# A Conformer block on one core: gated unit and convolution repacked as 128 + 16 channels, whole-chunk norms, and PSUM pairs reserved for ScalarE

## The chip, the core and the metric

The kernel runs on one core of a Trainium2 chip. The metric is device time in microseconds (us), as the median of a few executions. The engines are called as in the profile: PE is TensorE's matmuls, PEld its weight loads, DVE is VectorE, ACT is ScalarE, POOL is GpSimd.

Ratios are the mean time of one kernel's fast runs over that of the other's of the same rounds, so they are not quite the ratio of the medians quoted beside them.

## The reference

Two sequences of 4000 tokens with 144 channels go through one block, all in bf16:

```python
h = layernorm(x);  x = x + 0.5 * (silu(h @ w_ff1a) @ w_ff1b)          # 144 -> 576 -> 144
q, k, v = split(layernorm(x) @ w_qkv)                                  # 4 heads of 36
x = x + softmax(q @ k.T * 36**-0.5) @ v @ w_o                          # full attention, 4000 keys
a, b = split(layernorm(x) @ w_pw1)                                     # 144 + 144
c = depthwise_conv5(a * sigmoid(b), dw)                                # per channel, along tokens
x = x + silu(c) @ w_pw2
x = x + 0.5 * (silu(layernorm(x) @ w_ff2a) @ w_ff2b)
return layernorm(x)
```

## The kernel before

Tokens are cut into 16 chunks of 500 (eight for each sequence), and a chunk into four blocks of 125. Token `4p + i` of a chunk sits at position p of block i. Attention runs through 1008 **tiles**: 16 chunks of queries times 63 tiles of 64 keys, all four heads at once. A tile is one group of four score matmuls (128 partitions x 1000 columns of PSUM, two neighbouring banks), one exponential, and one group of four value matmuls.

An exponential is one ScalarE instruction over both banks, or, for some tiles, eight VectorE instructions that build the same from shifts and a polynomial. Of the eight PSUM banks two hold the attention's output, so six are shared by score tiles, which need a **pair**, and by all other work, which takes one bank at a time.

The order of instructions is fixed when the kernel is built. A recording layer keeps its own rough estimate of when each engine would be free, and a scheduler picks the next step from it; on the chip each engine then simply goes through its list, with semaphores. Three stages follow. The *start* runs up to the first exponential (first feed-forward, keys and values of the first chunk). The *body* is the stream of 1008 tiles, with the rest of the block filled in between. The *tail* comes after the last exponential.

The parts that the change touches (cuts marked):

```python
HD = 72                                   # 144 channels as two halves of 72 partitions
class Banks(Slots):
    def take(self):                       # one bank for any other work: anything nearly free
        t = min(self.free.values()) + 0.3
        ok = [i for i, f in self.free.items() if f <= t]
        i = min(ok, key=lambda j: ((j ^ 1) in self.free, self.free[j], j))
        del self.free[i]
        return i
    def take_pair(self): ...              # two neighbouring banks for a score tile

def ln_tr(c, s, g):                       # half a chunk (2 blocks): norm, transpose, copy
    u = yield from ln(c, g)
    yield from transp(XN[0:TB, u, :, :], ("XN", u), XT[0:HD, s, :, g*2*TB:(g+1)*2*TB], [("XT", s, g)])

def glu(c, s, hf):                        # spawned for hf = 0, 1
    bk, t = yield need("pe", (banks, thp), dur=0.42)
    mm2(WP1, s, D + hf * HD, D + (hf + 1) * HD, bk, HD, ["WP1"])      # 72 outputs x 500 tokens
    yield from tanh(bk, t, HD)                                        # 72x500 on ScalarE
    ...
    mm2(WP1, s, hf * HD, (hf + 1) * HD, bk, HD, ["WP1"])
    op("dve", "scalar_tensor_tensor", out=U[0:HD, c % NU, hf, :, 1:1 + TB], ...)   # 72x500

def conv(c, z, hf, silu):                 # spawned for hf = 0, 1: nine diagonal matmuls, 72 channels
    ...
    op("pe", "matmul", o[:, i0:i1, :], lhsT=DG[0:HD, hf, tap, :], rhs=u[:, s0:s0 + i1 - i0, off:off + TB], ...)
    yield from tanh(bk, t, HD)

def want_dve(n):                          # does VectorE take this tile's exponential?
    if not DVE_EXP or live_dve[0] >= 1 or t > NT - 6 or (t < 3 and c == 0) or len(kv_done) < CPB:
        return False
    return R.free["dve"] < R.free["pe"] + 0.6
```

The softmax here doesn't subtract the row's maximum and nothing guards it: scores larger than these inputs give would overflow.

## Time and profile before

| | busy, us | share of the 1075.4 us span |
|---|---|---|
| TensorE matmuls | 957.5 | 89% |
| VectorE | 913.5 | 85% |
| ScalarE | 938.5 | 87% |
| GpSimd | 363.6 | 34% |

The median time was 1079.0 us (three executions). The table does not name a bottleneck: three engines stand within 4 points. The next lines do. First, from the page of the kernel before: the busy share of ScalarE in 40 equal slices (tenths), and the shares of engines and lines in the chain of work that ended last.

```profile
ACT  3998789999889998999879899999999999999932
...
ACT 37%; PE 33%; DVE 16%; POOL 11%; issue 2%; DMA 1%; ACTq 0%; POOLq 0%; DVEq 0%
PE PS L155 33%; ACT PT L155 31%; POOL RS L155 6%; POOL XN L155 4%; ACT TH L155 4%; DVE ZB L155 4%; DVE MB L155 2%; DVE ST L155 2%; DVE X L155 2%; DVE HT L155 1%; DVE OTF L155 1%; DVE SW L155 1%; DMA WQKV<-in_w_qkv_dram 1%; DVE XT L155 1%; DVE PT L155 1%
```

The body is nearly full and both ends are not, so an average over the span mixes stages. The view of busy time by windows, cut at the first and after the last exponential (busy us, with the number of instructions in brackets; PEclk is TensorE's granted clock):

```profile
core 0: us, PE busy (x) PEld busy (x) DVE busy (x) ACT busy (x) POOL busy (x), PEclk, DMA share, GB/s
0.00:33.51 33.51, 27.98 (x212) 15.17 (x212) 24.00 (x126) 16.67 (x30) 12.96 (x35) 1.00 0.33 99
33.51:1025.63 992.12, 896.35 (x10796) 341.47 (x10797) 865.52 (x2153) 909.13 (x1095) 339.13 (x646) 0.99 0.01 4
1025.63:1075.40 49.77, 33.15 (x194) 21.80 (x191) 24.02 (x94) 12.71 (x22) 11.56 (x27) 0.63 0.03 10
```

ScalarE is busy 909.1 of the 992.1 us of the body, 91.6%, so it is idle for 83 us there. The groups of instructions (busy us, mean ns of one | idle us of the engine just before them and what ended it):

```profile
L155 ACT ACTIVATE PT<-PS 128x1000 bf16<-128x1000 f32 x885 | 829.1, 1024 | 76.4 <-PE PS L155 73.9
...
L155 DVE TENSOR_TENSOR PT<-ZB,MB 128x1000 bf16<-128x1000 bf16 x123 | 84.9, 690 | 2.9
...
L155 ACT ACTIVATE TH<-PS 128x500 bf16<-128x500 f32 x112 | 65.2, 612 | 1.0 <-PE PS L155 0.8
...
L155 ACT ACTIVATE TH<-PS 72x500 bf16<-72x500 f32 x60 | 35.2, 586 | 3.9 <-PE PS L155 3.8
```

ScalarE computes 885 tiles and VectorE 123 (the second line is the last of its eight instructions). 76.4 us of ScalarE's idle time stand before exponentials. The view of waits says for whom (us in total, times, longest us):

```profile
ACT PT L155 <- PE PS L155: 73.9, 121, 2.3
...
PE PS L155 <- ACT PT L155: 44.3, 154, 1.1
...
PE PS L155 <- POOL XN L155: 26.4, 32, 2.4
```

They wait for score matmuls. TensorE also waits for ScalarE, in the other direction: a new score tile needs a pair of banks that an exponential has not yet freed. And it waits 26.4 us for norms that GpSimd computes (`XN`).

TensorE's 89% is not a sign of a full engine. The Trainium skill (Perfetto Trace Analysis, "Identifying the Most-Contended Engine") says that the busy share of matmuls is a poor measure of how near the engine is to its limit, because they are pipelined, and points to the arithmetic rate and to the share of weight loads instead. This trace agrees with the first half: the matmuls of a score group show 392 ns each, but the timeline has the next group starting 0.21 to 0.24 us after the group's own start, as here:

```profile
645.60 0.41 PE L155 MATMUL PS<-QT,KT 64*64 64x500 bf16 x4
...
645.83 0.38 PE L155 MATMUL PS<-PT,VA 64*37 64x500 bf16 x4
```

The weight loads are busy for 35% of the span.

### The profile page before, as it was taken

To read this page: it belongs to the slowest core of one execution; us is meant where nothing else is said; L and a number is where in the kernel's file an instruction comes from. 1 tells how busy PE (TensorE), PEld (TensorE's weight loads), DVE (VectorE), ACT (ScalarE), POOL (GpSimd) and SP (SyncE) were. 2 spreads that over 40 slices of the span, in tenths; PEclk is the share of its full clock that TensorE was granted. 3 is DMA by queue.
4 is the path that set the end of the run, shared out by engine and by line. 5 is a ranking of instruction groups with operands and counts; after the bars stand their busy time and mean duration, and the time that the engine had idled before them with its cause. 6 is when DMAs were issued, how large, how long until landed. Compare 5 with 4: busy or idle time off the path is not lost.

```text
span 1075.4 us, 26861 instructions
## 1 busy us (share of the span) xinstructions
PE 957.5 (89%) x11198; PEld 378.4 (35%) x11198; DVE 913.5 (85%) x2372; ACT 938.5 (87%) x1147; POOL 363.6 (34%) x707
## 2 busy tenths in 40 slices
PE   8999989999999999998989998898989898888866
PEld 4444333333333344323433332223332333323244
DVE  6867988889989898888988999988889898878844
ACT  3998789999889998999879899999999999999932
POOL 4312343425442546223254153113123142324112
PEclk9999999999999999999999999999999999999966
DMA  4000000000000000000000000000000000000000
GB/s 124 2 2 1 2 2 1 2 2 5 4 2 2 7 2 7 4 5 2 1 7 7 1 7 5 4 1 7 2 2 7 2 7 1 7 2 8 1 6 12
DMA packets 8996, 7.32 MB, mean 7 GB/s; under 512 B 2298, under 2 KB 8874, under 8 KB 8874
## 3 DMA queue, kind: packets, MB, share of 16 engines
q1 hardware_dynamic: 7718, 5.13, 1.6%
q8 instruction: 88, 1.44, 0.6%
q10 hardware_dynamic: 1156, 0.47, 0.2%
q14 instruction: 34, 0.28, 0.1%
HBM read 3.30 MB, written 2.30 MB: 5 GB/s over the span
## 4 chain that ended last, share of the span: by engine, by line
ACT 37%; PE 33%; DVE 16%; POOL 11%; issue 2%; DMA 1%; ACTq 0%; POOLq 0%; DVEq 0%
PE PS L155 33%; ACT PT L155 31%; POOL RS L155 6%; POOL XN L155 4%; ACT TH L155 4%; DVE ZB L155 4%; DVE MB L155 2%; DVE ST L155 2%; DVE X L155 2%; DVE HT L155 1%; DVE OTF L155 1%; DVE SW L155 1%; DMA WQKV<-in_w_qkv_dram 1%; DVE XT L155 1%; DVE PT L155 1%
## 5 line engine op out<-in xcount | busy, mean ns | idle before, releaser
L155 ACT ACTIVATE PT<-PS 128x1000 bf16<-128x1000 f32 x885 | 829.1, 1024 | 76.4 <-PE PS L155 73.9
L155 PE MATMUL PS<-QT,KT 64*64 64x500 bf16 x4032 | 411.8, 392 | 46.8 <-ACT PT L155 31.6
L155 PE MATMUL PS<-PT,VA 64*37 64x500 bf16 x4032 | 373.8, 375 | 16.6 <-ACT PT L155 11.8
L155 POOL TENSOR_SCALAR RS<-MV 125x2 f32<-125x2 f32 x276 | 93.1, 337 | 573.7 <-DVE MV L155 559.2
L155 PEld LDWEIGHTS PS<-QT,KT 64*64 64x64 bf16 x4032 | 122.3, 104 | 295.1 <-ACT PT L155 197.4
L155 DVE TENSOR_SCALAR ZB<-PS 128x500 uint16<-128x500 f32 x246 | 154.7, 670 | 18.6 <-PE PS L155 17.3
L155 POOL TENSOR_SCALAR XN<-X,RS 125x144 bf16<-125x144 bf16 x232 | 136.2, 593 | 12.1
L155 PEld LDWEIGHTS PS<-PT,VA 64*37 64x37 bf16 x4032 | 106.1, 96 | 92.0 <-ACT PT L155 53.5
L155 POOL TENSOR_TENSOR RS<-RS,NHALF 125x2 f32<-125x2 f32 x160 | 127.6, 797 | 13.3
L155 ACT ACTIVATE TH<-PS 128x500 bf16<-128x500 f32 (+2 forms) x200 | 110.8, 575 | 5.6 <-PE PS L155 5.2
L155 DVE SCALAR_TENSOR_TENSOR HT<-TH,PS 128x500 bf16<-128x500 bf16 (+1 forms) x140 | 84.3, 616 | 30.4 <-ACT TH L155 29.4
L155 DVE TENSOR_SCALAR MB<-MB 128x1000 f16<-128x1000 f16 x246 | 102.3, 416 | 2.5
L155 DVE TENSOR_TENSOR PT<-ZB,MB 128x1000 bf16<-128x1000 bf16 x123 | 84.9, 690 | 2.9
L155 DVE TENSOR_TENSOR MB<-MB 128x1000 f16<-128x1000 f16 x123 | 83.3, 678 | 2.8
L155 PE MATMUL PS<-IDENT,XN 125*72 125x125 bf16 x512 | 52.1, 227 | 34.6 <-POOL XN L155 26.4
L155 DVE SCALAR_TENSOR_TENSOR X<-PS,X 125x288 bf16<-125x288 f32 x128 | 56.4, 449 | 26.7 <-PE PS L155 25.9
L155 DVE BATCH_NORM_STATS2 ST<-X 125x6 f32<-125x144 bf16 x320 | 77.4, 293 | 0.3
L155 PE MATMUL PS<-XT,WA 72*128 72x500 bf16 x256 | 73.9, 393 | 1.7 <-DVE HT L155 0.7
L155 DVE COPY XT<-PS 72x500 bf16<-72x500 bf16 x119 | 48.2, 410 | 31.0 <-PE PS L155 29.9
L155 PE MATMUL PS<-WB,HT 128*125 128x144 bf16 x640 | 61.3, 237 | 2.3 <-ACT HT L155 1.9
L155 PEld LDWEIGHTS PS<-IDENT,XN 125*72 125x72 bf16 x512 | 34.3, 115 | 77.0 <-POOL XN L155 49.7
L155 PE MATMUL PS<-U,DG 72*72 72x250 bf16 (+3 forms) x288 | 58.8, 311 | 1.8 <-POOL U L155 1.5
(68 smaller groups left out, 710.5 us busy)
## 6 DMA issues: line engine op xcount, KB each, us to landing
X<-in_x_dram SPq DMA_DIRECT2D x16, 140.6 KB
out_dram<-XN SPq DMA_DIRECT2D x32, 70.3 KB
WA<-in_w_ff1a_dram ACTq DMA_DIRECT2D x1, 144.0 KB
WB<-in_w_ff1b_dram ACTq DMA_DIRECT2D x1, 144.0 KB
WA<-in_w_ff2a_dram SPq DMA_DIRECT2D x1, 144.0 KB
WB<-in_w_ff2b_dram SPq DMA_DIRECT2D x1, 144.0 KB
WQKV<-in_w_qkv_dram ACTq DMA_DIRECT2D x1, 121.5 KB
WP<-in_w_pw_dram SPq DMA_DIRECT2D x1, 81.0 KB
```

The lines of the kernel that those rows point to most:

```text
L155: ins = getattr(eng, o.name)(*o.a, **o.k)
```

## The change

Its intent is to take work off ScalarE, VectorE and TensorE around the gated unit and the convolution, to shorten the instruction lists of norms and transposes, and to let nothing else take the PSUM pairs that keep ScalarE fed. Its core (cuts marked):

```diff
-def glu(c, s, hf):   ... 72 channels x 500 tokens, twice
+def glu(c, s):       # 128 channels x 500 tokens
+    mm2(WP1, s, D, D + ML, bk, ML, ["WP1"])
+    yield from tanh(bk, t, ML)
+    ...
+def glu_left(c, s):  # the 16 channels left over: block i lands on partitions 16i..16i+15
+    for ab in (1, 0):
+        for i in range(NB):
+            for k in range(2):
+                op("pe", "matmul", PSV[0:LP, bk, (1 - ab) * 128:(1 - ab) * 128 + TB],
+                   lhsT=WPZ[0:HD, k, ab, 48 - LC * i:128 - LC * i],     # weights between zeros
+                   rhs=XT[0:HD, s, k, i * TB:(i + 1) * TB], ...)
+    yield from tanh(bk, t, LP, TB)                                       # 80 partitions x 125
...
-def conv(c, z, hf, silu):   nine matmuls for each half of 72
+def conv(c, z, silu):       nine matmuls for 128 channels
+def conv_left(c, z, silu):  three matmuls of 125 columns: taps between blocks are in the weights
...
-def ln_tr(c, s, g):         half a chunk
+def ln_tr(c, s, bs):        parts(): whole chunks in the body, halves in start and tail
+    NXN = 5                 # buffers of a whole chunk; before: 8 of half a chunk
...
 class Banks(Slots):
+    def choose(self):       # a single bank only while two pairs are free or queued for ScalarE
+        ok = [i for i in self.free if self.pairs(i) + len(self.queued) >= self.keep]
+        ...
+        return min((i for i in ok if self.free[i] <= t), key=lambda j: (-self.pairs(j), self.free[j], j))
...
-            return ok[0]
+            return min(ok, key=lambda q: not q[2].req.hold)   # first what holds a bank or a buffer
...
+def lag():   # pacing: is other work behind the attention? then no tile for VectorE, and LATE more room
+    ...
 def want_dve(n):
-    return R.free["dve"] < R.free["pe"] + 0.6
+    return len(eq) + banks.pairs() >= KEEP and R.free["dve"] < R.free["pe"] + DSLACK and not lag()
+KEEP = 2; DSLACK = 0.6; PRELAG = 0.5; BMIN = 1.5; DRAIN = 0.6; LATE = 0.3; DGAP = 5.0
+def reserve():   # a third pair when a tile for VectorE is due (5 us after its last one)
```

Also changed: in the scheduler's model, the latency of the score matmuls and the costs of the value projections and of the norm's steps on VectorE and GpSimd; ranks of threads, one buffer instead of two for VectorE's tiles, five instead of two for attention outputs, the order of the four value matmuls, and the projection after the convolution (one matmul of 128 channels and one of the stacked 16 for each block, instead of two of 72).

## The prediction

> **What bounds the kernel now.** The page: TensorE 89%, VectorE 85%, ScalarE 87% of 1075.4 us. Cut by stage (busy time by windows), ScalarE is busy 16.7 of 33.5 us up to its first softmax exponential, 909.1 of the next 992.1 us (91.6%), and 12.7 of the last 49.8. The body is a stream of 1008 attention tiles: ScalarE takes 885 (one exponential 1024 ns, 937 ns of engine time), VectorE 123 (530 us, 4.3 us each). ScalarE is the bound; its 83 us idle in the body is the loss, nearly all exponentials waiting for score matmuls (waits: 73.9 us, 121 times). TensorE is busy on paper, but matmuls overlap: from issue intervals in the timeline (attention group of four 0.21 us, feed-forward matmul 0.21) I estimate 770 us of 992. It is late because other work holds PSUM pairs or because VectorE (865.5 of 992 in the body) frees banks late, not for lack of capacity.
>
> **What the change does**, by counting instructions of both programs:
> - ScalarE: 29 tiles come back from VectorE (885 to 914; VectorE 123 to 94). 500-wide tanh fall from 172 to 138, 30 of 125 columns are added, five silu go to the tail. For widths the trace lacks I use the Trainium skill (ScalarE: Activation LUTs, "What ACT_TABLE_LOAD costs"): 186 ns + 0.833 ns per column, about 93 ns of overlap; that gives 1019 ns for 1000 columns, the trace 1024. So +29 x 0.93, -34 x 0.50, +30 x 0.19, +2: **+17 us of ScalarE**, 938 to about 955.
> - VectorE: -29 x 4.3 = -125 us; 60 combining passes of 500 columns (0.67 us) become 30 of 500 and 30 of 125: -12; whole-chunk copies: about -9. **About -145 us**, 85% to about 73%.
> - TensorE: gated-unit and conv matmuls go from 72 to 128 output channels at the same cost, so the main parts halve; the 16 left over add 304 matmuls of 125 columns. Estimate -15 us, and 490 bursts of other work between attention groups instead of 518.
> - GpSimd: 145 instructions fewer; not critical.
> - Scheduling: single PSUM banks are given out only while two pairs are free or queued for ScalarE.
>
> So ScalarE's work grows. The gain can only come from its idle time: reserved pairs and a VectorE with a quarter of slack should let TensorE run ahead. I expect the body's ScalarE share to rise from 91.6% to about 95.5%: 921 us busy (some tanh move to the ends) / 0.955 = 964 us. The start stays near 35 us, the tail near 49 (half the conv matmuls, but one more chunk's feed-forward). Sum 1048; I predict **1046 us** (range **1024 to 1073**). Chances: faster by over 2% 0.68, within 2% 0.27, slower 0.05.
>
> **What would show it.** ScalarE busy 945 to 962 us; idle before exponentials from 76 to 25-45 us; VectorE near 73%; tanh 80x125 near 275 ns; body about 28 us shorter; tail within 3 us. In the chain of waits, ScalarE's share rises above 37%. If VectorE's relief is the cause, TensorE's waits on VectorE shrink; if the pairs are, its waits on exponentials shrink.
>
> **What would make it wrong.** (1) The order is fixed ahead by the kernel's own model; if its latencies are off, ScalarE stays near 92%: about 1079 us or more. (2) Two banks left for all else could starve the feed-forward chains and push work into the tail. (3) ScalarE above 97%: near 1030 us. (4) Whole-chunk norms lengthen chains; harmless unless the last chunks wait for them.

## The result and the profile after

| | before | after |
|---|---|---|
| median, us | 1079.7 (4 runs) | 1030.6 (4 runs, 1028.1 to 1031.8) |
| ratio | | 0.9543 (95%: 0.9516 to 0.9569) |
| start: up to the first exponential, us | 33.5 | 37.7 |
| body, us | 992.1 | 929.3 |
| ScalarE busy in the body, us (share) | 909.1 (91.6%) | 911.0 (98.0%) |
| ScalarE idle in the body, us | 83.0 | 18.3 |
| tail, us | 49.8 | 59.3 |
| tiles on ScalarE / VectorE | 885 / 123 | 914 / 94 |

The kernel became 49 us faster, and its output was correct. From the page of the changed kernel, the same lines as of before:

```profile
ACT  3899999999999999999999999999999999999741
...
ACT 65%; PE 22%; DVE 9%; POOL 2%; issue 1%; DMA 1%; ACTq 0%; POOLq 0%; DVEq 0%
ACT PT L158 59%; PE PS L158 22%; ACT TH L158 5%; DVE ZB L158 2%; DVE ST L158 1%; DVE MB L158 1%; DVE HT L158 1%; POOL RS L158 1%; DVE X L158 1%; POOL XN L158 1%; DMA WQKV<-in_w_qkv_dram 1%; DVE XT L158 1%; DVE PT L158 0%; DVE XN L158 0%; DVE MV L158 0%
```

The view of busy time by windows, cut in the same way:

```profile
core 0: us, PE busy (x) PEld busy (x) DVE busy (x) ACT busy (x) POOL busy (x), PEclk, DMA share, GB/s
0.00:37.69 37.69, 30.78 (x246) 17.27 (x246) 27.98 (x131) 18.24 (x34) 13.60 (x35) 1.00 0.31 89
37.69:966.99 929.30, 856.63 (x10822) 323.80 (x10822) 732.42 (x1852) 910.99 (x1112) 255.77 (x494) 1.00 0.01 4
966.99:1026.30 59.31, 37.43 (x229) 23.98 (x226) 27.63 (x110) 16.59 (x31) 13.97 (x34) 0.64 0.03 8
```

The groups of instructions, and after them the waits:

```profile
L158 ACT ACTIVATE PT<-PS 128x1000 bf16<-128x1000 f32 x914 | 851.9, 1041 | 11.5 <-PE PS L158 9.8
...
L158 ACT ACTIVATE TH<-PS 128x500 bf16<-128x500 f32 x138 | 84.1, 616 | 6.0 <-PE PS L158 5.7
...
L158 DVE TENSOR_TENSOR PT<-ZB,MB 128x1000 bf16<-128x1000 bf16 x94 | 66.0, 702 | 2.2
...
L158 ACT ACTIVATE TH<-PS 80x125 bf16<-80x125 f32 x30 | 8.6, 288 | 1.5 <-PE PS L158 1.5
```

```profile
PE PS L158 <- ACT PT L158: 37.9, 135, 1.0
...
ACT PT L158 <- PE PS L158: 9.8, 30, 1.0
...
PE PS L158 <- POOL XN L158: 2.0, 3, 1.0
```

ScalarE did *more* in the body than before, 911.0 against 909.1 us, and the body still lost 62.8 us. All of that is idle time: exponentials that waited 73.9 us for scores now wait 9.8. The chain of waits says the same: its share on ScalarE went from 37% to 65%, that of TensorE's PSUM groups from 33% to 22%.

Some of the gain went back at the ends: the start is 4.2 us longer and the tail 9.5 us. The sum is 4.2 - 62.8 + 9.5 = -49.1 us, the difference of the two spans.

The tail can be read further. The groups in the tail's window alone, first of the kernel before, then of the changed one:

```profile
L155 ACT ACTIVATE HT<-PS 128x500 bf16<-128x500 f32 x8 | 4.5, 587 | 4.7 <-PE PS L155 4.7
```

```profile
L158 ACT ACTIVATE HT<-PS 128x500 bf16<-128x500 f32 x12 | 7.0, 587 | 5.3 <-PE PS L158 5.2
```

Twelve full-width feed-forward activations stand in the tail instead of eight: a third chunk's second feed-forward was left over. The granted clock in the tail is 0.64 against 1.00 in the body; it was 0.63 before, so the clock is no reason for the tail's growth. The Trainium skill (TensorE: Matmul & The Clock Gate, "The HAM clock gate") says that the clock of TensorE is throttled by default and that sustained activity releases it; the traces agree, with 0.63 and 0.64 in tails where TensorE is busy for 67 and 63% of the time, and 0.99 to 1.00 in bodies where it is busy for 90 and 92%.

### The profile page after: what moved, and what is told of

The parts are those of the page before. It is cut to its first block, busy times and chain, and to the rows that moved or that the text cites. A ratio compares the mean times of both kernels' runs of the same rounds, so it can differ in the third digit from the quotient of the medians.

```text
span 1026.3 us, 26612 instructions
## 1 busy us (share of the span) xinstructions
PE 924.8 (90%) x11294; PEld 365.0 (36%) x11294; DVE 788.0 (77%) x2092; ACT 945.8 (92%) x1175; POOL 283.3 (28%) x562
## 4 chain that ended last, share of the span: by engine, by line
ACT 65%; PE 22%; DVE 9%; POOL 2%; issue 1%; DMA 1%; ACTq 0%; POOLq 0%; DVEq 0%
ACT PT L158 59%; PE PS L158 22%; ACT TH L158 5%; DVE ZB L158 2%; DVE ST L158 1%; DVE MB L158 1%; DVE HT L158 1%; POOL RS L158 1%; DVE X L158 1%; POOL XN L158 1%; DMA WQKV<-in_w_qkv_dram 1%; DVE XT L158 1%; DVE PT L158 0%; DVE XN L158 0%; DVE MV L158 0%
## 5 line engine op out<-in xcount | busy, mean ns | idle before, releaser
L158 ACT ACTIVATE PT<-PS 128x1000 bf16<-128x1000 f32 x914 | 851.9, 1041 | 11.5 <-PE PS L158 9.8
L158 PE MATMUL PS<-QT,KT 64*64 64x500 bf16 x4032 | 397.4, 391 | 50.3 <-ACT PT L158 29.5
L158 POOL TENSOR_SCALAR RS<-MV 125x4 f32<-125x4 f32 (+1 forms) x160 | 46.3, 289 | 668.3 <-DVE MV L158 662.7
L158 DVE TENSOR_SCALAR ZB<-PS 128x500 uint16<-128x500 f32 x188 | 118.5, 672 | 33.2 <-PE PS L158 31.9
L158 POOL TENSOR_TENSOR RS<-RS,NHALF 125x4 f32<-125x4 f32 (+1 forms) x103 | 97.6, 948 | 8.6
L158 DVE TENSOR_SCALAR MB<-MB 128x1000 f16<-128x1000 f16 x188 | 78.0, 415 | 1.5
L158 DVE TENSOR_TENSOR PT<-ZB,MB 128x1000 bf16<-128x1000 bf16 x94 | 66.0, 702 | 2.2
L158 DVE TENSOR_TENSOR MB<-MB 128x1000 f16<-128x1000 f16 x94 | 63.8, 679 | 2.1
L158 PEld LDWEIGHTS PS<-WB,HT 128*125 128x125 bf16 x640 | 49.4, 143 | 37.4 <-issue 22.6
L158 DVE COPY XT<-PS 72x1000 bf16<-72x1000 bf16 (+1 forms) x65 | 40.1, 617 | 11.7 <-PE PS L158 10.6
```

The costliest lines, as they stand in the source:

```text
L158: ins = getattr(eng, o.name)(*o.a, **o.k)
```

## The experiments

The profile shows *that* ScalarE is fed, not which part of the change feeds it. The theories:

- **A**: the two reserved pairs of PSUM banks do it; TensorE can always run ahead.
- **B**: the relief of VectorE does it (94 tiles instead of 123, 913.5 down to 788.0 us busy): banks that VectorE must free come back sooner.
- **C**: the packing of gated unit and convolution, the whole-chunk norms and the new priorities do it.

Every kernel gave the right output. Each was run four times; the kernel before, run beside them on the same chips, had medians of 1077.8 to 1079.7 us, and the ratios are to those runs. "Body" and "tail" are cut as above; the share is ScalarE's in the body.

| run | median, us | ratio to before | start | body | share | idle | tail | tiles on VectorE |
|---|---|---|---|---|---|---|---|---|
| before | 1079.7 | 1 | 33.5 | 992.1 | 91.6% | 83.0 | 49.8 | 123 |
| changed | 1030.6 | 0.9543 | 37.7 | 929.3 | 98.0% | 18.3 | 59.3 | 94 |
| 1 no reservation | 1039.2 | 0.9631 | 45.4 | 944.9 | 94.2% | 55.0 | 46.9 | 127 |
| 2 the same, fewer VectorE tiles | 1049.6 | 0.9730 | 47.2 | 954.7 | 95.8% | 40.3 | 46.6 | 96 |
| 3 before, fewer VectorE tiles | 1077.0 | 0.9982 | 34.8 | 992.4 | 93.7% | 63.0 | 49.1 | 97 |
| 4 before, reservation alone | 1070.1 | 0.9927 | 35.4 | 983.4 | 95.4% | 45.0 | 47.7 | 80 |
| 5 changed, old conv | 1055.0 | 0.9778 | 40.1 | 948.2 | 97.3% | 25.2 | 65.3 | 89 |
| 6 changed, half-chunk norms | 1038.0 | 0.9629 | 37.5 | 937.2 | 97.4% | 24.7 | 61.7 | 93 |
| 7 changed, no "holders first" | 1043.0 | 0.9667 | 40.7 | 941.3 | 97.1% | 27.3 | 62.0 | 93 |
| 8 before, new conv alone | 1069.2 | 0.9917 | 35.5 | 985.8 | 91.3% | 85.8 | 45.0 | 124 |
| 9 changed, LATE 0.15 | 1021.5 | 0.9474 | 39.6 | 934.4 | 98.4% | 15.3 | 47.4 | 85 |
| 10 changed, tuned a | 1018.5 | 0.9450 | 34.8 | 932.3 | 98.3% | 15.9 | 47.5 | 88 |
| 11 changed, tuned b | 1015.3 | 0.9417 | 37.2 | 931.5 | 98.4% | 14.5 | 46.9 | 89 |
| 12 changed, no pacing | 1046.6 | 0.9693 | 38.9 | 926.7 | 96.8% | 29.7 | 79.6 | 103 |

### 1. The changed kernel without the reservation

```diff
-    KEEP = 2
+    KEEP = 0
-        return KEEP + 1 if due else KEEP
+        return KEEP
```

With `KEEP` at 0 VectorE's tiles need no free pairs either, and no third pair is kept for them.

> The changed kernel with the reservation of PSUM pairs switched off, nothing else edited; by count VectorE then takes 127 of the 1008 tiles (94 in the changed kernel), ScalarE 881. Theory A (the two reserved pairs keep ScalarE fed): ScalarE's share of the body, 98.0% in the changed kernel, falls back to 91 to 94%, the waits of exponentials for score matmuls grow from 9.8 to over 40 us, and with 31 us less ScalarE work than the changed kernel the time is 1040 to 1065 us. Rival B (the relief of VectorE did it): also slower, because VectorE gets its 33 tiles back and is busy again 85% or more; same numbers. Rival C (packed conv, whole-chunk norms and priorities did it): ScalarE stays at 97% or more and the time is at or under 1030 us.

The body in the view by windows (columns as above), then the group of exponentials:

```profile
45.35:990.24 944.89, 865.26 (x10826) 336.13 (x10824) 852.50 (x2108) 889.91 (x1082) 265.99 (x494) 1.00 0.01 4
```

```profile
L158 ACT ACTIVATE PT<-PS 128x1000 bf16<-128x1000 f32 x881 | 824.0, 1032 | 52.3 <-PE PS L158 50.7
```

ScalarE's share fell to 94.2% and its waits for scores rose from 9.8 to 50.7 us, as theory A said. But the whole kernel lost only 8.6 us (1030.6 to 1039.2), which is just under A's range of 1040 to 1065. Without the reservation VectorE took 33 tiles more, which saved ScalarE 21 us of work in the body (889.9 against 911.0). So most of the 49 us does *not* depend on the reservation. With the rest alone the kernel is already 40 us under the one before, although C's numbers (a share of 97% or more, 1030 us at most) were wrong. The stages moved in different directions: start 7.7 us longer (at a granted clock of 0.86 instead of 1.00), body 15.6 us longer, tail 12.4 us shorter, without the third chunk's feed-forward in it.

### 2. The same, with VectorE's tiles limited

```diff
-        ... < R.free["pe"] + DSLACK and not lag()
+        ... < R.free["pe"] + DSLACK and not lag() and R.free["pe"] > last_dve[0] + 8.0
```

(on top of the edit of run 1)

> As the run before, without reservation, but VectorE may take a tile only 8 us after its last one: 96 tiles, nearly the 94 of the changed kernel, so VectorE has the same slack and ScalarE the same work. Theory A (pairs): ScalarE's share of the body stays at 92 to 95%, body 960 to 990 us, time 1050 to 1080 us. Rival B (VectorE's slack): share 97 to 98%, body 930 to 940 us, time 1018 to 1035 us. Rival C: as B.

```profile
47.24:1001.98 954.74, 869.83 (x10839) 331.66 (x10839) 732.73 (x1862) 914.46 (x1114) 252.65 (x494) 1.00 0.01 4
```

That is the body's row. With VectorE's load as in the changed kernel (732.7 against 732.4 us in the body) ScalarE stays at 95.8%, not at 98.0%. B's range (1018 to 1035 us) is missed by far; A's time (1050 to 1080) by 0.4 us, its share (at most 95%) by 0.8 points and its body (at least 960 us) by 5.3 us. At nearly equal division of tiles, the reservation is worth 25 us of the body and 19 us of the kernel, for the start is 9.5 us longer without it (clock 0.89) and the tail 12.7 us shorter.

### 3. The kernel before, with VectorE's tiles limited

```diff
-        return R.free["dve"] < R.free["pe"] + 0.6
+        return R.free["dve"] < R.free["pe"] + 0.6 and R.free["pe"] > last_dve[0] + 8.0
```

> The kernel before, with VectorE limited in the same way to 97 tiles instead of 123, so ScalarE gets 26 more exponentials (24 us). Rival B (VectorE's slack feeds ScalarE): the body's share rises from 91.6% to 96 to 98%, time 1030 to 1050 us, faster than before. Theory A: share at most 94%, the added work is not paid back, time 1075 to 1100 us. VectorE falls from 85% to about 75% of the span either way.

```profile
34.80:1027.22 992.42, 897.71 (x10806) 340.56 (x10807) 766.05 (x1947) 929.45 (x1121) 324.71 (x646) 0.99 0.01 4
```

VectorE's work in the body fell from 865.5 to 766.1 us and the body's length did not move (992.1, 992.4). ScalarE's idle time fell by 20 us, from 83.0 to 63.0, and its work rose by the same 20 us, from 909.1 to 929.5. The median moved by 1.8 us, and the interval of the ratio (0.9952 to 1.0012) contains 1. B is refuted as a cause that works alone: slack on VectorE does feed ScalarE better, but it is bought with the tiles that ScalarE has to take over.

### 4. The kernel before, with the reservation alone

```diff
+    (choose(), pairs(), queued, keep as in the change)
+        banks.keep = 2            # before every choice, until the tail
-        return R.free["dve"] < R.free["pe"] + 0.6
+        return len(eq) + banks.pairs() >= 2 and R.free["dve"] < R.free["pe"] + 0.6
```

> The kernel before with the reservation alone (a single PSUM bank is given out, and a tile given to VectorE, only while two pairs are free or queued for ScalarE); conv, norms, transposes, priorities and latencies as before. By count VectorE then takes 80 tiles, ScalarE 928 (43 more, 40 us of work). Theory A: the body's share rises from 91.6% to 96 to 98%, idle before exponentials falls from 76 us to under 35, and the time is 1045 to 1068 us although ScalarE has more work than in either kernel. Rival C (the rest of the change is needed): share 93% or less, time 1085 to 1115 us.

ScalarE's share is 95.4%, near A's range (96 to 98%), and the time of 1070.1 us lies just above A's (1068 at most); C's numbers (93% or less, 1085 us or more) are missed too. VectorE takes only 80 tiles here, so this run has reserved pairs *and* a VectorE with slack. The timeline at the longest wait, all of it ScalarE waiting (start, length in us; the bracket is the idle time before):

```profile
597.29 0.58 ACT L155 ACTIVATE TH<-PS 72x500 bf16<-72x500 f32 x1 [0.81 <-PE PS L155]
...
603.42 1.85 PE L155 MATMUL PS<-XTQ,WK 72*128 72x500 bf16 x4 [0.51 <-DVE XTQ L155]
...
605.19 1.30 PE L155 MATMUL PS<-WQKV,XTQ 72*64 72x72 bf16 x36
...
609.69 1.05 PE L155 MATMUL PS<-QT,KT 64*64 64x500 bf16 x8
...
610.37 1.90 ACT L155 ACTIVATE PT<-PS 128x1000 bf16<-128x1000 f32 x2 [12.50 <-PE PS L155]
```

For 12.5 us ScalarE has no scores at all. In this gap TensorE projects keys (`XTQ,WK`), values (`WQKV`) and queries, and the first scores follow at once. Counted by score groups, it is the 55th of the second sequence's tiles, the first that needs keys of that sequence's last chunk: the work that prepares them is late. The kernel before waits 0.5 us at most around this tile, so here the reservation, the only edit, brought the stall. But run 8, without any reservation, waits 5.9 us at the same tile, so this is a weak point of the order that other edits hit too. Without that one wait the share would be 938.4 / (983.4 - 12.5) = 96.7%. In the rest of the body the reservation works, then; the work that prepares the next keys has to be kept on time.

### 5. The changed kernel with the old gated unit and convolution

```diff
-        kids = S.spawn((glu(c, s2), glu_left(c, s2)))
+        kids = S.spawn(glu(c, s2, hf) for hf in range(2))       # glu, conv, weights of before
-    NAN = 5
+    NAN = 3       # for space; alone it changes only addresses in the built program
```

> The changed kernel with the gated unit and the convolution of before (two halves of 72 channels), all else as changed (the attention-output buffers cut from 5 to 3 for space, which by itself leaves the order of instructions as it is). By count ScalarE has 5 more exponentials and 30 more 500-wide tanh, minus 30 of 125: about +14 us of work at 0.93, 0.50 and 0.19 us. Theory C (the packing is a main part of the gain, its work saved turns into time one for one on the bound engine): time 1043 to 1052 us, the body's ScalarE share still 97 to 98%. Theory A (reservation is nearly all): at most 1036 us. VectorE busy about the same, since it takes 5 tiles less.

```profile
40.06:988.24 948.18, 873.03 (x10714) 324.36 (x10714) 721.92 (x1804) 922.97 (x1116) 252.82 (x465) 1.00 0.01 4
988.24:1053.50 65.26, 45.23 (x241) 29.41 (x239) 28.18 (x110) 17.88 (x32) 13.68 (x31) 0.57 0.02 7
```

The loss is 24.4 us, more than C's range. The body is 18.9 us longer, of which 12.0 us are ScalarE's work (923.0 against 911.0; 14 were estimated) and 6.9 us idle time. The tail is 6.0 us longer; it has twice the main convolution matmuls and a clock of 0.57, and what each of the two adds was not separated. The start takes the other 2.4 us of the two spans' difference.

### 6. The changed kernel with half-chunk norms, and 7. without "holders first"

```diff
-        return [range(0, 2), range(2, 4)] if mode["front"] or mode["tail"] else [range(0, 4)]
+        return [range(0, 2), range(2, 4)]              # run 6; eight half-size buffers
```

```diff
-            return min(ok, key=lambda q: not q[2].req.hold)
+            return ok[0]                               # run 7; likewise for VectorE
```

> The changed kernel with norms, transposes and copies by half chunks throughout, as before (eight half-size norm buffers). ScalarE's work is unchanged (915 exponentials, 93 tiles on VectorE); GpSimd gets some 170 instructions more, VectorE some 50. Theory: whole-chunk norms matter little in the body because neither VectorE nor GpSimd bounds it; share 97% or more, time within 1% of the changed kernel, 1022 to 1041 us. Rival: the longer instruction lists of VectorE and PE's extra switches delay score matmuls: share under 96.5%, time over 1041 us.

> The changed kernel without the scheduler's new preference for work that holds a PSUM bank or a buffer (the choice on TensorE and VectorE goes back to the first in the list). Counts nearly equal (93 tiles on VectorE). Theory: with only two banks for everything else, releasing them first matters: banks are held longer, other work falls behind and the tail or the body grows by 5 to 15 us, time 1035 to 1046 us. Rival: no effect, 1025 to 1035 us.

Both are as expected: 7.4 and 12.4 us slower. In neither does ScalarE's work move by more than 3 us (912.5 and 914.0 us); the idle time of the body rises from 18.3 to 24.7 and 27.3 us, and the tail by 2 to 3 us. Our reading, which no view shows directly, is that the lists get longer or worse ordered and other work reaches its banks later.

### 8. The kernel before with the new gated unit and convolution alone

```diff
-        kids = S.spawn(glu(c, s2, hf) for hf in range(2))
+        kids = S.spawn((glu(c, s2), glu_left(c, s2)))           # glu, conv, weights of the change
```

> The kernel before with the gated unit and convolution as 128 channels plus the stacked 16, nothing else of the change. By count 884 exponentials, 142 tanh of 500 and 30 of 125, VectorE 124 tiles: ScalarE's work falls by about 10 us, TensorE's by about 15. Theory C: the share of the body stays near 91.6%, so the time falls by 10 to 18 us, to 1061 to 1070 us. Theory A: under 5 us, since the idle time, not the work, is the loss.

8.6 us are gained, a little under the 10 to 18 that C gave, with a time (1069.2 us) at the weak end of its range. The body shrinks by 6.3 us (ScalarE's work falls by 9.2, its idle time rises by 2.8) and the tail by 4.8 us. The longest wait for scores is at the tile of run 4's stall:

```profile
617.67 1.90 ACT L158 ACTIVATE PT<-PS 128x1000 bf16<-128x1000 f32 x2 [5.93 <-PE PS L158]
```

The same packing that costs 24.4 us when taken out of the changed kernel gives 8.6 us when put into the one before.

### 9 to 11. Can the tail be had back?

```diff
-    LATE = 0.3
+    LATE = 0.15        # run 9: how much other work that lags may delay a score matmul
```

> The changed kernel with one constant of its scheduler halved (the extra lateness that other work may cause to a score matmul while that work lags, 0.3 to 0.15). By count VectorE takes 85 tiles instead of 94 (ScalarE 9 more exponentials, 8 us), and the feed-forward of the third last chunk, which the changed kernel leaves to the tail, is finished before the last exponential (20 silu instead of 25). Theory (the tail grew from 49.8 to 59.3 us because of that chunk's work at a low granted clock): tail back to 46 to 50 us, body 932 to 940 us, time 1020 to 1029 us. Rival (the tail's growth has another cause, such as the leftover matmuls or the whole-chunk chains): tail stays at 56 us or more, time 1032 us or more.

The tail's row by windows, and the activations in it:

```profile
973.94:1021.30 47.36, 31.96 (x202) 21.80 (x200) 24.61 (x96) 13.83 (x27) 12.30 (x30) 0.59 0.04 10
```

```profile
L158 ACT ACTIVATE HT<-PS 128x500 bf16<-128x500 f32 x8 | 4.4, 590 | 3.3 <-PE PS L158 3.3
```

Eight activations again, and 47.4 us, as the theory said. But run 10 below is the counterexample. It leaves a third chunk's feed-forward in the tail too, and its tail is as short:

```profile
967.05:1014.50 47.45, 31.91 (x216) 21.31 (x216) 23.63 (x93) 16.06 (x30) 14.16 (x35) 0.71 0.04 10
```

```profile
L158 ACT ACTIVATE HT<-PS 128x500 bf16<-128x500 f32 x12 | 6.7, 587 | 5.0 <-PE PS L158 5.0
```

So the amount left over does not lengthen the tail by itself; the timelines point to where it stands in the order. In run 10 the leftover feed-forward comes first, 6.5 to 10 us after the last exponential, and the last activation of a convolution starts 24 us after it (26 us in the kernel before). In the changed kernel that activation starts only after 38 us, behind the feed-forwards of two chunks. In run 9, then, the way was free again; that this is the whole reason was not tested.

The body of run 9 is 5.1 us longer for nine tiles more on ScalarE; the kernel gains 9.1 us (1030.6 to 1021.5).

```diff
# run 11 (run 10 is of the same kind)
-    NXN = 5;  NAN = 5;  DSLACK = 0.6;  PRELAG = 0.5;  BMIN = 1.5;   DRAIN = 0.6;  LATE = 0.3;   DGAP = 5.0;  PW = 0.12
+    NXN = 6;  NAN = 2;  DSLACK = 0.4;  PRELAG = 1.0;  BMIN = 1.75;  DRAIN = 0.3;  LATE = 0.15;  DGAP = 6.0;  PW = 0.08
```

> Six norm buffers instead of five (in the start and the tail each holds half a chunk only, and the kernel before had eight of that size) and seven scheduler constants moved a little. 88 tiles on VectorE. Expected: first exponential at 33 to 36 us instead of 37.7, body 930 to 938 us, tail 46 to 52 us, time 1015 to 1027 us; if the number of norm buffers is not what delays the start, it stays at 37 us or later.

> As the run before with other constants; 89 tiles on VectorE, and the third last chunk's feed-forward finished in the body (20 silu). Expected: first exponential at 33 to 36 us, body 930 to 938 us, tail 46 to 50 us, time 1015 to 1027 us.

```profile
L158 ACT ACTIVATE PT<-PS 128x1000 bf16<-128x1000 f32 x919 | 855.8, 1045 | 7.8 <-PE PS L158 6.7
```

Run 11 is the fastest kernel: 1015.3 us, 5.8% under the kernel before and 15 us under the changed one, with 6.7 us of waits for scores. Its start of 37.2 us missed the expectation, while run 10, with the same six norm buffers, starts at 34.8 us. The granted clock in the start was 1.00 in run 10 and 0.86 in run 11, so what the sixth buffer is worth stays open.

### 12. The changed kernel without pacing

```diff
 def lag():
-    if len(kv_done) < CPB:
-        return False
+    return False
```

> The changed kernel with the pacing switched off: the rule that gives other work more room, and VectorE no attention tiles, once that work lags behind the attention, is made never to apply. By count VectorE takes 103 tiles (94), and a fourth chunk's feed-forward is left to the tail (30 silu, 25 in the changed kernel, 20 before). Theory (two reserved pairs starve the other work unless something paces it, as the 12.5 us stall at the batch boundary in the fourth run suggests): ScalarE's work in the body falls by some 10 us, but a wait of several us appears where the second batch starts, and the tail grows from 59 to 70 us or more; time 1037 to 1055 us. Rival (the pacing does little): no wait over 2 us in the body, time 1022 to 1033 us.

The tail's row by windows, then the timeline at the longest wait in the body:

```profile
965.62:1045.20 79.58, 53.20 (x296) 34.55 (x296) 32.69 (x134) 22.48 (x43) 20.86 (x49) 0.58 0.03 10
```

```profile
566.58 1.01 PE L158 MATMUL PS<-XTQ,WK 72*128 72x500 bf16 x4
...
569.18 0.62 PE L158 MATMUL PS<-QT,KT 64*64 64x500 bf16 x8
...
569.63 1.90 ACT L158 ACTIVATE PT<-PS 128x1000 bf16<-128x1000 f32 x2 [5.61 <-PE PS L158]
```

The numbers are as expected: at the tile where runs 4 and 8 stall (not at the very start of the second sequence), ScalarE's exponentials wait 5.6 us behind the projections of keys and queries, and the tail grows to 79.6 us. The pacing is worth this much, then. That the reserved pairs are what makes it necessary is not shown: no run of the changed kernel is without both, and in run 4, with pairs and no pacing, the tail did not grow (47.7 us, 49.8 before). The median rises by 15.9 us although ScalarE had 14 us less to do in the body (897.0 against 911.0).

## Why the prediction was right, and where it was not

The time (1046 predicted, 1030.6 measured) lies in the range, and where it saw the gain was right: ScalarE gets more work, and the gain is its idle time. Which parts of the change bring it was right only in part. What came is case (3) of its own list of failures, "ScalarE above 97%: near 1030 us", and a part of case (2), work pushed into the tail. Point by point:

- **"The body's ScalarE share to rise from 91.6% to about 95.5%"** was the mis-sized term: it rose to 98.0%. With 911 us of work instead of the 921 assumed, the body took 929 us, not 964, an error of 35 us. The idle time left was 18.3 us, where the sum had 43 (964 - 921).
- **"The tail near 49"** was wrong: 59.3 us. The step weighed "half the conv matmuls" against "one more chunk's feed-forward" and called it even. By runs 5 and 8 the convolution is worth about 5 or 6 us there. Run 9, without that chunk, has a tail 12 us shorter; run 10 keeps the chunk and is as short, so calling it even was not absurd; the order in the tail is what differs. The start was 37.7 us, not 35. Together 13 us, which by luck hid a part of the first error.
- **"+17 us of ScalarE"** was 7.3 us (938.5 to 945.8). Summed by group the work did grow as counted, by 17.5 us (977.1 to 994.6); but in the engine's busy time instructions that overlap count once, and more of them overlap now. The mean length of an exponential fits, which rose from 1024 to 1041 ns. The width for which the trace had no length was nearly right: for 80x125 the prediction said 275 ns and 288 were measured; the skill's formula (ScalarE: Activation LUTs, "What ACT_TABLE_LOAD costs") gives 290.
- **"About -145 us" of VectorE** was -125.5. The groups that were costed changed as predicted (-124 us for the tiles, -12 for combining passes, -8 for copies, summed by group); the busy time of the engine as a whole, in which overlapping instructions count once, fell less.
- **"Reserved pairs and a VectorE with a quarter of slack"** named two causes. Slack on VectorE alone gives nothing (run 3), and the reservation alone 8.7 us (run 4). Run 4 has both named causes at once, and still only 8.7 of the 49 us. The prediction gave no weight of its own to the priorities (12.4 us when taken out) or the whole-chunk norms (7.4 us), and called the latter "harmless". The pacing (15.9 us) it did not name; its failure case (2) describes what happens without it.
- **"GpSimd: … not critical"** overlooked the chain of waits, where GpSimd held 11% before and 2% after. TensorE's waits for GpSimd's norms fell from 26.4 to 2.0 us. No single part that was tried explains all of it: put into the kernel before, they leave 20.7 (run 3), 13.5 (run 4) and 23.3 us (run 8), and without any one of them the changed kernel has at most 5.1. The costs of the norm's steps in the scheduler's model are a rival that was not run: one `XN` step stood there as 0.50 us, now 0.55, and took 0.59 in the trace before.
- **TensorE's convolution "at the same cost"** for 128 outputs as for 72 is borne out: by the median distance from the start of a 72x500 matmul to that of the next of its group, one with 128 outputs (feed-forward) took 221 ns and one with 72 (gated unit) 238 ns in the trace before.
- **The proposed test between the two causes did not work.** "TensorE's waits on VectorE shrink" or "on exponentials shrink": the first rose from 20.5 to 32.5 us (all lines of the view added), the second fell only from 44.3 to 37.9 us, and neither view separates the causes. Waits of an engine that has time to spare do not show what the bound engine gained.

Taken out of the changed kernel, the parts cost 24.4 (packing), 15.9 (pacing), 12.4 (holders first), 8.6 (reservation) and 7.4 us (whole-chunk norms). This adds up to 69 us, more than the 49 gained; the two put in alone gave 8.6 and 8.7. So the parts support one another, and no share of the 49 us belongs to one of them. Our reading, argued and not shown, is this: a reservation keeps ScalarE fed at the price of the other work's banks; packing, whole-chunk steps and "holders first" make that work use banks for less time, and pacing keeps it from falling behind.

One caution: every edit reorders the whole list of instructions. Constants and buffer counts alone moved the time by 9 to 15 us (runs 9 to 11), so an effect of that size is that of an edit together with its new order. What the changed latencies and costs, the ranks and the order of value matmuls do was not tried, and stays open.

## What to carry to other kernels

Cut the profile at the stages of the bound engine before adding up busy time: here a kernel whose averages named no bottleneck had an engine that lost 83 us in one stage, and the change that won gave it *more* work. When a scarce resource is reserved for the bound engine, look at once whether other work falls behind: here such waits stood at the first tile that needs the last keys of a sequence (12.5 us in run 4), and pacing the other work was worth 15.9 us. Look at what is left for the tail and where it stands in the order there: a third chunk's feed-forward went with a tail of 59.3 us in the changed kernel and of 47.5 us in run 10.

## What the Trainium skill lacked or had wrong

- Perfetto Trace Analysis, "Identifying the Most-Contended Engine": nothing wrong here. It takes the engine with the highest busy share as the one to optimise first, but judges TensorE by its weight loads (35 and 36% here). That picks ScalarE, by 87 to VectorE's 85% over the whole span; in the body the margin is clear, 91.6 to 87.2% before and 98.0 to 78.8% after.
- The same page, "Optimization Strategy": it says that consistent gaps on the engine that should be full can mean too little PSUM for the next tile. That agrees: without reserved banks the waits for scores rose from 9.8 to 50.7 us (run 1), and to 36.5 at nearly the same division of tiles (run 2). It lacks the reverse, that PSUM held back for one engine can delay the very work that feeds it: 12.5 us without scores in run 4, where the reservation was the only edit (though 5.9 us at the same tile in run 8, without one).
- TensorE: Matmul & The Clock Gate: it gives no mean granted clock for a kernel's first stage. In our profiles that of the first 34 to 47 us lay between 0.82 and 1.00, so small differences between starts may be the clock's; how much it adds was not measured.
- No page that we found gives GpSimd's power operation. `125x2` took 722 ns and `125x4` 1131 ns in the changed kernel, so one whole-chunk call costs less than two half-chunk ones.
